# Expert 0 of a mixture-of-experts kernel: the half tile of rows turned with all 128 rows, and the turns between the second products of tiles 3 and 4 placed later

## The chip, the cores and the metric

The kernel runs on one core of one Trainium2 chip. The metric is the device time of one execution in microseconds (us). Three timed runs of the kernel before gave 525.79, 527.39 and 529.98 us, median 527.39 us; the profiled execution described below took 526.51 us.

## The reference

An attention layer with gates (8 heads of 40, 4 sequences of 768 steps) makes 3072 rows of 320 numbers. Those rows go through a mixture of 8 experts, two per row. All arithmetic is fp32.

```
logits = x @ w_gate
noisy_logits = logits + np.log1p(np.exp(x @ w_noise)) * noise
top2 = np.argpartition(-noisy_logits, 2, axis=1)[:, :2]
...
for e in range(E):
    for k in range(2):
        mask = top2[:, k] == e
        h = np.maximum(x[mask] @ w1[e], 0.0)          # 320 -> 1024
        out[mask] += top2_w[mask, k, None] * (h @ w2[e])   # 1024 -> 320
```

What the change touches lies in expert 0's part: picking its rows, turning them so that TensorE can contract over the 320 features, and the second product `h @ w2`.

## The kernel before

The first 130 us or so compute the attention in 24 units of 128 rows and write the rows to memory (`rows`). The routing of the last units runs on VectorE while expert 0 has already begun. After that, TensorE goes through experts 0 to 7 in program order.

Every fp32 product is made from parts: an operand is split into a high part and a low part (`xh` and `xl` for the rows, `w1h`/`w1l` and `w2h`/`w2l` for the weights, `hx` for both parts of the hidden values), and three products are summed in PSUM.

**Tiles.** An expert's rows lie in `XG`, tile t of 128 rows in `XG[:, t]`. Expert 0 and a few others have 832 rows: tiles 0 to 5 are full and tile 6 has 64 rows (`rows_of(6)` is 64). Expert 0 is worked in three pieces, as its rows become known: tiles 0 to 2, tiles 3 and 4, tiles 5 and 6. `XG` has no second copy: expert 1's tile t is gathered into the place of expert 0's. All of `XG` was set to zero early in the kernel (line 898).

**Gather (line 781).** GpSimd issues one indirect DMA per tile, which picks the tile's rows from memory by a list of row numbers (`tok`). In the stretch of the change seven are issued in a row: expert 0's tiles 5 and 6, then expert 1's tiles 0, 1, 2, 3 and 4. The same queue of GpSimd has carried expert 1's weights shortly before (lines 1135 and 1136).

**Turn (`transpose_x`, lines 807 to 816).** Three matmuls against the identity (`cs`) turn one tile's 3 x 128 feature columns into a PSUM bank (line 811). ScalarE copies the bank to `xh` (line 813), then VectorE subtracts for the low parts (lines 814 and 815), which frees the bank. The banks for turns come in the order `xt`, `s0`, `xt`, `s1` (function `bank`, line 738); there is one `xt` bank, and two buffers each of `s0` and `s1`. Tile 6 is turned with 64 rows and 64 columns.

**First product (`mm1`, line 1006).** For each of 8 blocks f of 128 hidden values, eight matmuls; ScalarE applies the relu and writes the high part (line 1017), VectorE the low part (line 1020).

**Second product (`mm2`, lines 1029 to 1050).** For one tile, 8 blocks j, each of three matmuls with 320 columns (lines 1036, 1037, 1038) into bank `o` or `st`. Block j needs the hidden values of f = j from ScalarE and VectorE. The argument `between` names a tile to turn behind block j. At the end VectorE scales the bank into `y` (line 1049), and `put` issues a scatter-add of `y` to the output from GpSimd (line 1059). A tile of 64 rows has 8 blocks of two matmuls (lines 1044 and 1045).

**Order.** Each engine works through its own instructions in the order written here. In the stretch of the change that order is, on TensorE: `mm1` of tiles 3 and 4, `mm2(0, 3)` into bank `o` with three turns between its blocks, `mm2(0, 4)` into bank `st` with two, `mm1` of tiles 5 and 6 with two turns, `mm2(0, 5)`, the turn of expert 1's tile 5, `mm2(0, 6)`, the turn of expert 1's tile 6, and then `mm1` of expert 1. In line 1149 the number before a colon is the block j behind which the turn stands, the number after it the tile: 5 and 6 are expert 0's tiles, 0, 1 and 2 are already expert 1's.

Of the kernel before, what the change touches and what calls it, by code (L numbers as in the profile page):

```python
# [64 lines left out]
def build(ctx, tc, qk, vk, og, fi, noise, wgn, w1, w2, cst, ce, out):  # L65
    nc = tc.nc
    V, A, P, T, SP = nc.vector, nc.scalar, nc.gpsimd, nc.tensor, nc.sync
# [11 lines left out]
    ident = cs[:, C_ID:C_ID + 128]  # L79
# [47 lines left out]
    XG = early.tile([128, 7, RW], F32, name="xg")  # L127
# [276 lines left out]
    CB3 = (0, 128, DM - 128)  # L404
# [17 lines left out]
    def l_part(i):  # L422

        t = XTB if i < NU else psum.tile([128, 512], F32, name="st")
        u = i - 2
        if 0 <= u < NU:
            for j in range(3):
                T.matmul(t[:, LGC:LGC + 16], XS[u][:, j, :], wgt[:, j, :], start=(j == 0), stop=(j == 2))
        return t
# [303 lines left out]
    def bank(use):  # L733

        n = dict(h=("s0", "s1", "e"), x=("xt", "s0", "xt", "s1"), y=("st", "o"))[use]
        turn[use] += 1
        name = n[turn[use] % len(n)]
        return psum.tile([128, 512], F32, name=name, bufs=2 if name in ("s0", "s1") else 1)
# [22 lines left out]
    def token(e, t):  # L761
        return TOK[0:rows_of(t), TC * e + t:TC * e + t + 1]
# [3 lines left out]
    def weigh(e, h=None):  # L766

        if not h:
            GW[e] = rt.tile([128, 7], F32, name="gw", bufs=2)
            GW[e, 2] = rt.tile([128, 7, 2], F32, name="gw2", bufs=2)  # L770
        t = tiles(e, h)
        n = slice(t[0], t[-1] + 1)
        V.tensor_mul(GW[e, 2][:, n], XG[:, n, DM:DM + 2], KM[:, TC * e + n.start:TC * e + n.stop])
        V.tensor_add(GW[e][:, n], GW[e, 2][:, n, 0], GW[e, 2][:, n, 1])
# [23 lines left out]
    def tiles(e, h=None):  # L798
        if h is None:
            return range(7 if is_long(e) else 6)  # L800
        c = parts(e)[h]
        return range(c.start // 128, -(-c.stop // 128))

    def rows_of(t):
        return 128 if t < 6 else 64

    def transpose_x(t, b=None):
        n = rows_of(t)
        ps = (bank("x") if b is None else b).rearrange("p (j t) -> p j t", j=4)[:, 0:3]
        for j in range(3):  # L810
            T.transpose(ps[:, j, 0:n], XG[0:n, t, CB3[j]:CB3[j] + 128], ident[0:n, 0:n])
        c = slice(128 * t, 128 * t + n)
        A.activation(XH[:, :, c], ps[:, :, 0:n], AF.Copy)  # L813
        V.tensor_sub(XL[:, :, c], ps[:, 0:2, 0:n], XH[:, 0:2, c].bitcast(F32))
        V.tensor_sub(XH[0:64, 2, c], ps[64:128, 2, 0:n], XH[64:128, 2, c].bitcast(F32))  # L815
# [7 lines left out]
    while i < NU - LEAD:  # L823
# [48 lines left out]
        t = l_part(i)  # L872
# [45 lines left out]
    for t, name in zip(tiles(0, 0), ("s", "e", "st")):  # L918
        shape = [128, 2, 512] if name == "s" else [128, 512]
        b = psum.tile(shape, F32, name=name, bufs=2 if name == "s" else 1)  # L920
        transpose_x(t, b[:, 0] if name == "s" else b)
    t = l_part(u)
# [9 lines left out]
    t = l_part(u)  # L932
# [96 lines left out]
    def mm2(e, t, b="y", between={}):  # L1029
        n = rows_of(t)  # L1030
        ps = bank(b)[:, 0:DM]
        y = m2.tile([128, DM], F32, name="y", bufs=TA + 1)
        if n == 128:
            c = slice(128 * t, 128 * t + 128)
            for j in range(8):
                T.matmul(ps, HH[:, j, c], W2H[:, j], start=j == 0, stop=False)  # L1036
                T.matmul(ps, HH[:, j, c], W2L[:, j], start=False, stop=False)  # L1037
                T.matmul(ps, HLO[:, j, c], W2H[:, j], start=False, stop=j == 7)  # L1038
                if j in between:
                    transpose_x(between[j])  # L1040
        else:

            for j in range(8):
                T.matmul(ps, HT[:, j], W2H[:, j], start=j == 0, stop=False)
                T.matmul(ps, HT[:, j], W2L[:, j], start=False, stop=j == 7)
            A.activation(y[0:n], ps[n:128], AF.Copy)
            V.tensor_add(y[0:n], y[0:n], ps[0:n])
            ps = y
        V.tensor_scalar(y[0:n], ps[0:n], GW[e][0:n, t:t + 1], None, op0=OP.mult)  # L1049
        return y  # L1050
# [4 lines left out]
    def put(e, t, y):  # L1055
        n = rows_of(t)

        P.memset(gap, 0.0)
        st = P.indirect_dma_start(out=out, out_offset=bass.IndirectOffsetOnAxis(ap=token(e, t), axis=0),  # L1059
                                  in_=y[0:n], in_offset=None, compute_op=OP.add)  # L1060
        for o in puts.setdefault(e, []):
            tc.declare_no_dep(st.ins, o.ins, reason="an expert has a token once")
        puts[e].append(st)
# [55 lines left out]
    for k, (l, r) in enumerate(((HH, W2H), (HLO, W2H), (HH, W2L))):  # L1119
        for n in range(24):  # L1120
            t, j = divmod(n, 8)
            T.matmul(sums[t], l[:, j, 128 * t:128 * t + 128], r[:, j], start=k == 0 and j == 0, stop=k == 2 and j == 7)
            if k == 1 and n % 4 == 0 and 4 <= n < 20:
                low_w2(n // 4 + 3)
            if n % 2:
                wipe()
                advance((0.27, 0.0, 0.27 if n < 14 else 0.0)[k])
            if k == 2 and j == 7:
                held[t] = m2.tile([128, DM], F32, name="y", bufs=TA + 1)
                A.activation(held[t], sums[t], AF.Copy, scale=GW[0][:, t:t + 1])  # L1130
            if k == 2 and n in (14, 19):
                transpose_x(tiles(0, 1)[n // 19])
# [13 lines left out]
    gather(1, ts=tiles(0, 1))  # L1146
    for t in tiles(0, 1):
        put(0, t - 3, held[t - 3])
        put(0, t, mm2(0, t, "y", {0: 5, 3: 6, 6: 0} if t == 3 else {2: 1, 5: 2}))
    weigh(0, 2)  # L1150
    gather(1, ts=tiles(0, 2))
    side = split_w1(V)
# [10 lines left out]
    for t in tiles(0, 2):  # L1163
        y = mm2(0, t)
# [84 lines left out]
    with tc.If(most > NT):  # L1249
# [23 lines left out]
        with tc.If(most > BLK):  # L1273
            V.memset(ec, 0.0)
            with tc.For_i(0, NE, 1) as e:
                weights(e)
                with tc.For_i(0, NCH, 1) as c:
# [8 lines left out]
                    for r in range(2):  # L1286
                        x = xf[:, DM * r:DM * r + DM]
                        t = XD.rearrange("(r c p) d -> r c p d", r=2, c=NCH)[r, bass.ds(c, 1)]
# [88 lines left out]
```

## Time and profile before

| | |
|---|---|
| median of three timed runs | 527.39 us (525.79 to 529.98) |
| the profiled execution, its own time | 526.51 us |
| its span, first to last instruction | 524.7 us (1.8 us lie around it) |
| TensorE busy | 504.5 us of the span |
| VectorE, ScalarE, GpSimd busy | 339.6, 247.8, 228.0 us |
| granted TensorE clock, mean | 0.983 |

PE is TensorE's matmul stream and PEld its weight loads, DVE is VectorE, ACT ScalarE, POOL GpSimd. In a timeline row stand the start in us from the beginning of the span, the length, the engine, the line, the operation with what it writes and reads, the shape, and how many were merged; a bracket gives the idle time of the engine just before and what ended it. The end of a matmul is modelled by the profiler, so the step between starts is the better measure of what one costs. Tile names lose their numbers in the profile, so `s` stands for both `s0` and `s1`.

### The profile page before, as it was taken

The numbers are of one execution on the slowest core, as the hardware profiler recorded it, in microseconds if no ns is written. First come the engines' busy times: TensorE is split into PE (matmuls) and PEld (weight loads), VectorE is DVE, ScalarE is ACT, GpSimd is POOL, SyncE is SP. The second block draws the span as 40 slices with busy tenths as digits, with TensorE's granted clock in tenths as the row PEclk, the third lists the DMA queues.
The fourth block names the chain that finished last, engine by engine and source line by source line (L and its number), as shares of the span: only waits on it lengthen the run. The fifth ranks groups of instructions, "written<-read, shape, count | busy, mean of one in ns | idle before, by whom it ended". The sixth has DMA issues, their size and how long they took to land.

```text
span 524.7 us, 13163 instructions
## 1 busy us (share of the span) xinstructions
PE 504.5 (96%) x5052; PEld 476.1 (91%) x5053; DVE 339.6 (65%) x963; ACT 247.8 (47%) x567; POOL 228.0 (43%) x298
## 2 busy tenths in 40 slices
PE   8899998999999899999999999999999999999993
PEld 4788887988988898999999999999999999999993
DVE  7787989999897476854764584376548347545310
ACT  8678877888623255432541454054325415515300
POOL 7356665365114657055315714550562254151042
PEclk9589999999999999999999999999999999999998
DMA  5788787777758446078239406831861593272033
GB/s 161 189 235 258 203 237 210 209 207 223 270 194 256 91 66 211 17 186 204 62 78 277 94 19 152 215 91 48 251 109 51 112 247 85 64 166 25 2 39 41
DMA packets 51669, 76.80 MB, mean 146 GB/s; under 512 B 10809, under 2 KB 42048, under 8 KB 51600
## 3 DMA queue, kind: packets, MB, share of 16 engines
q1 hardware_dynamic: 38816, 50.32, 32.3%
q0 software_dynamic: 12784, 25.57, 23.3%
q8 instruction: 42, 0.69, 0.5%
q14 instruction: 27, 0.22, 0.1%
HBM read 52.27 MB, written 17.48 MB: 133 GB/s over the span
## 4 chain that ended last, share of the span: by engine, by line
PE 78%; DVE 12%; ACT 5%; DMA 2%; issue 1%; POOL 0%; SPq 0%; POOLq 0%; DVEq 0%
PE s L1006 23%; PE e L1006 11%; PE o L1037 5%; PE o L1036 5%; PE o L1038 5%; PE st L1037 5%; PE st L1036 5%; PE st L1038 5%; PE o L385 3%; DVE p L362 2%; PE s L348 2%; PE e L325 2%; DVE ob L639 2%; PE st L376 1%; DVE kd L356 1%
## 5 line engine op out<-in xcount | busy, mean ns | idle before, releaser
L1059 POOL DMA_INDIRECT y_out<-y,tok x53 | 87.1, 1643 | 190.7 <-DVE y L1049 190.0
L1017 ACT ACTIVATE hx<-s 128x384 fp32r<-128x384 f32 (+5 forms) x91 | 44.4, 488 | 108.1 <-PE s L1006 67.1
L1006 PE MATMUL s<-xh,w1h 128*128 128x384 f32 (+5 forms) x273 | 76.7, 338 | 0.0
L1020 DVE SCALAR_TENSOR_TENSOR hx<-s,hx 128x384 fp32r<-128x384 f32 (+3 forms) x91 | 48.1, 529 | 37.5 <-ACT hx L1017 31.5
L781 POOL DMA_INDIRECT xg<-rows,tok x53 | 57.8, 1090 | 24.2 <-issue 14.3
L1006 PE MATMUL s<-xh,w1l 128*128 128x384 f32 (+5 forms) x273 | 62.5, 336 | 0.1
L1037 PE MATMUL o<-w2l,hx 128*128 128x320 f32 x184 | 57.3, 312 | 0.0
L1036 PE MATMUL o<-w2h,hx 128*128 128x320 f32 x184 | 57.1, 310 | 0.0
L1038 PE MATMUL o<-w2h,hx 128*128 128x320 f32 x184 | 56.6, 307 | 0.0
L1037 PE MATMUL st<-w2l,hx 128*128 128x320 f32 x176 | 54.9, 312 | 0.0
L1036 PE MATMUL st<-w2h,hx 128*128 128x320 f32 x176 | 54.5, 310 | 0.0
L1038 PE MATMUL st<-w2h,hx 128*128 128x320 f32 x176 | 54.1, 307 | 0.0
L1006 PEld LDWEIGHTS s<-xh,w1h 128*128 128x128 f32 x273 | 48.9, 188 | 1.7 <-ACT xh L813 0.3
L1006 PEld LDWEIGHTS s<-xh,w1l 128*128 128x128 f32 x273 | 47.9, 188 | 1.7 <-DVE xh L815 0.3
L1017 ACT ACTIVATE hx<-e 128x384 fp32r<-128x384 f32 (+5 forms) x45 | 22.1, 491 | 52.4 <-PE e L1006 34.1
L1006 PE MATMUL s<-xl,w1h 128*128 128x384 f32 (+5 forms) x182 | 46.4, 336 | 0.0
L1049 DVE TENSOR_SCALAR y<-o,gw 128x320 f32<-128x320 f32 x23 | 12.7, 550 | 46.5 <-PE o L1038 46.4
L1049 DVE TENSOR_SCALAR y<-st,gw 128x320 f32<-128x320 f32 x22 | 12.1, 550 | 43.8 <-PE st L1038 43.8
L397 POOL TENSOR_TENSOR xr<-tm,vk 128x320 f32<-128x320 f32 x24 | 20.9, 872 | 41.2 <-ACT w L328 14.3
L1006 PE MATMUL e<-xh,w1h 128*128 128x384 f32 (+5 forms) x135 | 38.6, 340 | 0.0
L1038 PEld LDWEIGHTS o<-w2h,hx 128*128 128x128 f32 x184 | 34.7, 188 | 0.0
L1036 PEld LDWEIGHTS o<-w2h,hx 128*128 128x128 f32 x184 | 34.6, 188 | 0.1
(237 smaller groups left out, 1255.2 us busy)
## 6 DMA issues: line engine op xcount, KB each, us to landing
raw<-w_in SPq DMA_DIRECT2D x6, 1280.0 KB
qk<-qk_in SPq DMA_DIRECT2D x24, 256.0 KB
raw<-w_in SPq DMA_DIRECT2D x6, 1024.0 KB
y_out<-zrow SPq DMA_DIRECT2D x15, 320.0 KB
raw<-w_in SPq DMA_DIRECT2D x17, 256.0 KB
vk<-vk_in POOLq DMA_DIRECT2D x24, 162.0 KB
vk<-vk_in SPq DMA_DIRECT2D x24, 162.0 KB
vk<-og_in SPq DMA_DIRECT2D x24, 160.0 KB
```

What stands on the lines that cost most here:

```text
L325: T.matmul(ps, LE[j][0:KE, c, 64 - 64 * p:192 - 64 * p], RE[j][0:KE, p, :, c * L:c * L + L], start=True, stop=True)
L385: T.matmul(OQ[u][half[p], h, :], PP[u][n, p, h, :], VK[u % 4][p][n, h * 41:h * 41 + 41], start=True, stop=True)
L397: P.tensor_mul(XR[u], tm.rearrange("p h d -> p (h d)"), SG[u % 4])
L781: P.indirect_dma_start(out=XG[0:rows_of(t), t], out_offset=None, in_=XD[0:n], in_offset=bass.IndirectOffsetOnAxis(ap=token(e, t), axis=0), ...
L1006: T.matmul(ps[:, 0:n], l, r, start=i == 0, stop=i == len(ops) - 1)
L1017: A.activation(hi, x, AF.Relu)
L1020: V.scalar_tensor_tensor(lo, top[0], 0.0, top[1].bitcast(F32), op0=OP.max, op1=OP.subtract)
L1036: T.matmul(ps, HH[:, j, c], W2H[:, j], start=j == 0, stop=False)
L1037: T.matmul(ps, HH[:, j, c], W2L[:, j], start=False, stop=False)
L1038: T.matmul(ps, HLO[:, j, c], W2H[:, j], start=False, stop=j == 7)
L1049: V.tensor_scalar(y[0:n], ps[0:n], GW[e][0:n, t:t + 1], None, op0=OP.mult)
L1059: st = P.indirect_dma_start(out=out, out_offset=bass.IndirectOffsetOnAxis(ap=token(e, t), axis=0), in_=y[0:n], in_offset=None, compute_op= ...
```

## The change

Two edits in expert 0's code, nothing else. The turn of any tile uses all 128 rows and 128 columns of `XG[:, t]`; only tile 6 had fewer before. ScalarE and VectorE still read just the 64 columns that hold rows. And the turns inside the second products of tiles 3 and 4 move: in tile 3 from behind blocks 0, 3 and 6 (tiles 5, 6 and expert 1's 0) to behind blocks 4 and 7 (tiles 5 and 6); in tile 4 from behind blocks 2 and 5 (expert 1's tiles 1 and 2) to behind blocks 1, 3 and 5 (expert 1's tiles 0, 1 and 2).

```
         for j in range(3):
-            T.transpose(ps[:, j, 0:n], XG[0:n, t, CB3[j]:CB3[j] + 128], ident[0:n, 0:n])
+            T.transpose(ps[:, j], XG[:, t, CB3[j]:CB3[j] + 128], ident)
...
     for t in tiles(0, 1):
         put(0, t - 3, held[t - 3])
-        put(0, t, mm2(0, t, "y", {0: 5, 3: 6, 6: 0} if t == 3 else {2: 1, 5: 2}))
+        put(0, t, mm2(0, t, "y", {4: 5, 7: 6} if t == 3 else {1: 0, 3: 1, 5: 2}))
```

No engine gets more or fewer instructions; GpSimd's and the DMA queues' order is the same. On TensorE, at the start of the second product of tile 3 before the change (`o` is its bank, `s1_3361` and `xt_3377` are the turned tiles 5 and 6; a bracket names the engines or DMA queues whose signals the instruction waits for):

```order
L1036 MATMUL o_3356<-w2h_121,hx_2802 128x320 [waits DVE_49,Activation_49]
L1037 MATMUL o_3356<-w2l_123,hx_2802 128x320
L1038 MATMUL o_3356<-w2h_121,hx_2802 128x320
L811 MATMUL s1_3361<-cs_66,xg_122 128x128 [waits DMASW7_49,DVE_49]
L811 MATMUL s1_3361<-cs_66,xg_122 128x128 x2
L1036 MATMUL o_3356<-w2h_121,hx_2802 128x320 [waits Activation_49]
```

The same turn in the changed kernel stands behind the fifth block, and that of tile 6 (`xt_3389`, now 128 columns) behind the last, right ahead of tile 4's product in bank `st`:

```order
L1036 MATMUL o_3356<-w2h_121,hx_2802 128x320 [waits Activation_49]
L1037 MATMUL o_3356<-w2l_123,hx_2802 128x320
L1038 MATMUL o_3356<-w2h_121,hx_2802 128x320 [waits DVE_49]
L811 MATMUL s1_3373<-cs_66,xg_122 128x128 [waits DMASW7_49]
L811 MATMUL s1_3373<-cs_66,xg_122 128x128 x2
...
L1038 MATMUL o_3356<-w2h_121,hx_2802 128x320 [waits DVE_49]
L811 MATMUL xt_3389<-cs_66,xg_122 128x128 [waits DMASW0_49,PE_49]
L811 MATMUL xt_3389<-cs_66,xg_122 128x128 x2
L1036 MATMUL st_3401<-w2h_121,hx_2802 128x320
```

The turn of tile 5 waits for the DMA queue that its gather uses; four more blocks now stand ahead of it. In tile 4's product after the change, `s0_3409` and `xt_3422` are expert 1's tiles 0 and 1:

```order
L1038 MATMUL st_3401<-w2h_121,hx_2802 128x320
L811 MATMUL s0_3409<-cs_66,xg_122 128x128 [waits DMASW1_49]
L811 MATMUL s0_3409<-cs_66,xg_122 128x128 x2
L1036 MATMUL st_3401<-w2h_121,hx_2802 128x320
L1037 MATMUL st_3401<-w2l_123,hx_2802 128x320
L1038 MATMUL st_3401<-w2h_121,hx_2802 128x320
L1036 MATMUL st_3401<-w2h_121,hx_2802 128x320
L1037 MATMUL st_3401<-w2l_123,hx_2802 128x320
L1038 MATMUL st_3401<-w2h_121,hx_2802 128x320
L811 MATMUL xt_3422<-cs_66,xg_122 128x128 [waits DMASW2_49,DVE_49,Activation_49]
L811 MATMUL xt_3422<-cs_66,xg_122 128x128 x2
```

Between the two turns that share bank `xt` (tile 6, then expert 1's tile 1) stand four blocks and one turn now; before the change it was seven blocks and one turn. On VectorE the scaling of tile 3's result (line 1049) came behind the low parts of tile 6 and of expert 1's tile 0 (`s0_3393`):

```order
L814 TENSOR_TENSOR xl_2668<-xt_3377,xh_2667 128x2x64 [waits Activation_49]
L815 TENSOR_TENSOR xh_2667<-xt_3377,xh_2667 64x64
L814 TENSOR_TENSOR xl_2668<-s0_3393,xh_2667 128x2x128 [waits Activation_49]
L815 TENSOR_TENSOR xh_2667<-s0_3393,xh_2667 64x128
L1049 TENSOR_SCALAR y_3357<-o_3356,gw_2806 128x320 [waits PE_49]
```

After the change it stands between them, so that it no longer waits for expert 1's tile 0:

```order
L814 TENSOR_TENSOR xl_2668<-xt_3389,xh_2667 128x2x64 [waits Activation_49]
L815 TENSOR_TENSOR xh_2667<-xt_3389,xh_2667 64x64
L1049 TENSOR_SCALAR y_3357<-o_3356,gw_2806 128x320
L814 TENSOR_TENSOR xl_2668<-s0_3409,xh_2667 128x2x128 [waits Activation_49]
L815 TENSOR_TENSOR xh_2667<-s0_3409,xh_2667 64x128
```

## Rows read from the trace of the kernel before

**Rows 1.** The page's head, its first part (busy time, share of the span, instructions) and the first line of its fourth (the chain of work that ended last, by engine).

```profile
span 524.7 us, 13163 instructions
PE 504.5 (96%) x5052; PEld 476.1 (91%) x5053; DVE 339.6 (65%) x963; ACT 247.8 (47%) x567; POOL 228.0 (43%) x298
PE 78%; DVE 12%; ACT 5%; DMA 2%; issue 1%; POOL 0%; SPq 0%; POOLq 0%; DVEq 0%
```

**Rows 2.** Busy time by stretch: the stretch and its length, then busy us and instructions of PE, PEld, DVE, ACT and POOL, the granted clock, the DMA engines' busy share, GB/s.

```profile
165.00:169.00 4.00, 4.00 (x37) 4.00 (x36) 3.07 (x18) 1.53 (x4) 2.07 (x2) 1.00 1.01 330
169.00:172.00 3.00, 1.52 (x13) 1.29 (x12) 0.85 (x2) 0.40 (x2) 2.19 (x3) 1.00 0.34 100
176.00:181.00 5.00, 4.39 (x33) 4.15 (x32) 2.67 (x8) 1.70 (x4) 2.18 (x3) 1.00 0.41 70
181.00:186.00 5.00, 5.00 (x48) 5.00 (x47) 4.60 (x20) 2.22 (x7) 4.31 (x6) 1.00 0.54 67
215.00:300.00 85.00, 85.00 (x527) 83.37 (x526) 47.76 (x120) 31.23 (x65) 37.78 (x39) 1.00 0.56 140
400.00:500.00 100.00, 100.00 (x626) 100.00 (x625) 53.80 (x116) 37.23 (x79) 28.10 (x31) 1.00 0.39 92
```

**Rows 3.** TensorE's timeline through the second products of tiles 3 and 4, from the last matmul of the first product to the next first product.

```profile
169.09 0.28 PE L1006 MATMUL s<-xh,w1h 128*128 128x256 f32 x1
169.21 0.31 PE L1036 MATMUL o<-w2h,hx 128*128 128x320 f32 x1
...
169.50 0.31 PE L1038 MATMUL o<-w2h,hx 128*128 128x320 f32 x1
171.29 0.52 PE L811 MATMUL s<-cs,xg 128*128 128x128 f32 x3 [1.48 <-DMA xg<-rows,tok]
171.56 0.39 PE L1036 MATMUL o<-w2h,hx 128*128 128x320 f32 x1
...
172.54 0.31 PE L1036 MATMUL o<-w2h,hx 128*128 128x320 f32 x1
...
173.07 0.40 PE L811 MATMUL xt<-cs,xg 64*128 64x64 f32 x3
173.40 0.41 PE L1036 MATMUL o<-w2h,hx 128*128 128x320 f32 x1
...
173.94 0.31 PE L1036 MATMUL o<-w2h,hx 128*128 128x320 f32 x1
...
174.38 0.31 PE L1036 MATMUL o<-w2h,hx 128*128 128x320 f32 x1
...
174.83 0.49 PE L811 MATMUL s<-cs,xg 128*128 128x128 f32 x3
175.08 0.39 PE L1036 MATMUL o<-w2h,hx 128*128 128x320 f32 x1
...
175.60 0.31 PE L1036 MATMUL st<-w2h,hx 128*128 128x320 f32 x1
...
176.78 0.31 PE L1038 MATMUL st<-w2h,hx 128*128 128x320 f32 x1
177.70 0.52 PE L811 MATMUL xt<-cs,xg 128*128 128x128 f32 x3 [0.61 <-ACT xh L813]
177.97 0.39 PE L1036 MATMUL st<-w2h,hx 128*128 128x320 f32 x1
...
180.60 0.36 PE L1006 MATMUL e<-xh,w1h 128*128 128x192 f32 x2
```

**Rows 4.** The gather of tile 5 in the chain of work that ended last: start, us, what (for a DMA from its issue to its landing).

```profile
166.53 4.63 DMA xg<-rows,tok
```

**Rows 5.** GpSimd's timeline: the first and the last of the seven gathers issued in a row, of tile 5 and of expert 1's tile 4 (the third to the fifth of them are expert 1's tiles 0 to 2).

```profile
166.53 1.06 POOL L781 DMA_INDIRECT xg<-rows,tok  x1 [5.86 <-DVE over L662]
...
174.46 1.01 POOL L781 DMA_INDIRECT xg<-rows,tok  x1 [0.30 <-issue]
```

**Rows 6.** ScalarE's timeline: the relu of the last block ahead of tile 3's second product, the copies of the turned tiles 5 and 6, and the copy of expert 1's tile 2.

```profile
170.88 0.38 ACT L1017 ACTIVATE hx<-s 128x256 fp32r<-128x256 f32 x1 [1.86 <-PE s L1006]
172.39 0.49 ACT L813 ACTIVATE xh<-s 128x384 fp32r<-128x384 f32 x1 [1.12 <-PE s L811]
176.70 0.33 ACT L813 ACTIVATE xh<-xt 128x192 fp32r<-128x192 f32 x1 [3.82 <-PE o L1038]
...
179.91 0.49 ACT L813 ACTIVATE xh<-s 128x384 fp32r<-128x384 f32 x1 [0.81 <-PE s L811]
```

**Rows 7.** VectorE's timeline: the two instructions for the low parts of tile 6, the second of which frees bank `xt`.

```profile
177.06 0.29 DVE L814 TENSOR_TENSOR xl<-xt,xh 128x128 fp32r<-128x128 f32 x1 [3.42 <-ACT xh L813]
177.37 0.23 DVE L815 TENSOR_TENSOR xh<-xt,xh 64x64 fp32r<-64x64 f32 x1
```

**Rows 8.** TensorE's timeline: the turn of expert 1's tile 2 (128 rows), and the turn of expert 1's tile 6 (64 rows) with its neighbours.

```profile
179.39 0.49 PE L811 MATMUL s<-cs,xg 128*128 128x128 f32 x3
...
194.29 0.31 PE L1044 MATMUL st<-w2h,hx 128*128 128x320 f32 x1
194.44 0.31 PE L1045 MATMUL st<-w2l,hx 128*128 128x320 f32 x1
194.68 0.40 PE L811 MATMUL s<-cs,xg 64*128 64x64 f32 x3
195.00 0.73 PE L1006 MATMUL s<-xh,w1h 128*128 128x512 f32 x2
```

## The prediction

> **What bounds the kernel now.** I read the page's head and chain first: TensorE is busy for 504.5 of 524.7 us and holds 78% of the chain that ended last [rows 1]. So a change counts here by what it does to TensorE's stream. The busy time by stretch then shows where that stream has holes. From 181 us on there are none that the stretches shown would reveal (5.00 of 5.00, 85.00 of 85.00, 100.00 of 100.00); the stretch 169 to 172 has 1.52 us busy out of 3, and 176 to 181 has 4.39 out of 5 [rows 2]. Both lie in the second products of tiles 3 and 4, which the change rearranges. The timeline names them: ahead of the turn of tile 5 the engine sat idle until a gather landed, and ahead of the turn of expert 1's tile 1 until ScalarE's copy of line 813, because both that turn and tile 6's use the one bank `xt` [rows 3].
>
> The steps between starts give the prices. A block of three matmuls takes 174.38 - 173.94 = 0.44 us. Without a wait the turn of tile 5 would have started one third of a block after 169.50, at 169.65; it started at 171.29, so the first wait costs 1.64 us. In the same way the second costs 177.70 - 176.93 = 0.77 us [rows 3]. The reader should see that the idle times in brackets (1.48 and 0.61) are smaller, since the modelled end of a matmul lies about 0.16 us behind the next possible start.
>
> **Edit 1, 128 rows for tile 6.** A turn of 128 rows put between blocks stretches the step around it from 0.44 to 0.70 us (174.38 to 175.08) and the next from 0.44 to 0.52 (175.08 to 175.60), so it costs 0.34. The 64-row turn stretches them to 0.86 (172.54 to 173.40) and 0.54 (173.40 to 173.94) and costs 0.52 [rows 3]. Its own three matmuls take less (0.40 against 0.49); it loses more at its edges. Turned with 128 rows it gives 0.18 us. The same holds for expert 1's tile 6: from the end of the step after 194.44, at 194.59, to 195.00 it takes 0.41, against 0.26 for the full turn up to the next block [rows 3, 8], so 0.15 more. Nothing is added elsewhere: ScalarE and VectorE read the same 64 columns, and the other 64 rows were zeroed long before, so there is no new wait.
>
> The Trainium skill speaks against this edit: TensorE: Matmul & The Clock Gate, section Back-to-back issue gap, has the step of a matmul grow with its columns (columns / 2.4 ns plus 2.5 at the full clock). As an estimate from that page, 64 more columns would cost 3 x 27 ns = 0.08 us per turn and the edit would lose 0.16 us in all. The trace bears the page out for the three matmuls alone, and not for the stream around them.
>
> **Edit 2, the turn of tile 5 four blocks later.** TensorE now issues five blocks from 169.21 before it: 169.21 + 5 x 0.443 = 171.42 (0.443 is the mean step of 0.44 before rounding). The gather landed at 166.53 + 4.63 = 171.16 [rows 4], so the 1.64 us are covered by work that had to be done anyway, with 0.26 us to spare. If the gather landed later by more than that, the rest would be a wait again. The blocks that move ahead need the hidden values of f up to 4 first, and f = 7 last; the last relu was done at 171.26 [rows 6], and block 7 comes at about 172.6. No hole there.
>
> **Edit 2, the other turns.** The schedule without waits: tile 6 at 171.42 + 0.34 + 3 x 0.443 = 173.09, expert 1's tile 0 at 174.32, tile 1 at 175.54, tile 2 at 176.77, the next first product at 178.0, against 180.60 before. Are the rows there? Tile 6 was turned at 173.07 without a DMA wait, so it is. The seven gathers were issued (174.46 - 166.53) / 6 = 1.32 us apart [rows 5]. With tile 5's 4.63 us as an estimate for each, expert 1's tiles 0, 1 and 2 land at 173.8, 175.1 and 176.4: ahead of their turns by 0.5, 0.4 and 0.3. I take this as an upper bound of the landing, since tile 5 was issued while the DMA engines were full (share 1.01 up to 169) and the later ones when they were not (0.34) [rows 2]. Bounds: no wait, or some tenths.
>
> Is bank `xt` free at 175.54? It was freed 177.60 - 176.70 = 0.90 us after ScalarE's copy began [rows 6, 7], and the next turn came 0.10 later. An undisturbed copy begins 0.52 us after its turn (179.39, 179.91) [rows 6, 8], so the bank needs 1.52 us; the two turns stand 2.45 us apart. Then the 0.77 us go too, with 0.9 to spare. The catch is that tile 6's copy did not begin 0.52 us after its turn, but 3.63 us (173.07, 176.70), though ScalarE was idle for 3.82 us [rows 3, 6]. TensorE's signal came late. That is the open price, and it decides between the first case and the first rival.
>
> **Sum.** 1.64 + 0.77 + 0.18 + 0.15 = 2.74 us less. All of it passes to the end, since TensorE has no later hole to swallow it. The granted clock is 1.00 (2.4 GHz) in the stretch with the wait as in its neighbours [rows 2], so the clock neither gives nor takes. GpSimd's scatter of tile 3 waits for line 1049, which moves forward; expert 1's later gathers stand behind that scatter and can only come earlier. The profiled execution took 526.51 us; 526.51 - 2.74 = 523.8. The median of the three runs lies 0.88 above it, and I forecast against the median: 527.39 - 2.74 = **524.7 us**.
>
> **Rivals.** *The late signal comes again.* Three signals in a row were late here: the relu at 170.88 (1.79 us after 169.09), tile 5's copy (1.10), tile 6's (3.63). The first was late ahead of any 64-row turn, which speaks for something in this stretch of time that the change leaves alone. Against it: the third and longest follows the 64-row turn, which goes. If tile 6's copy begins at 176.70 again, bank `xt` is free at 177.60, the turn of tile 1 starts at 177.70 as before, but with four blocks behind it in place of five: 0.44 is gained there (tile 6's 0.18 is lost in the wait), 0.15 at expert 1's tile 6, 0.6 in all: 526.8. From a copy that begins 1.45 us after its turn on (2.45 - 1.00), each us is one us of wait.
>
> *A gather lands later.* The slack is 0.26 us for tile 5 and 0.3 to 0.5 by estimate for three others. A landing 1 us later gives 0.74 back: 525.4. For it: the queue was full of weights just before. Against it: nothing ahead of the gather changes.
>
> *The wider turns lose.* If the edges that I charged to 64 rows belong to their neighbours, edit 1 gives nothing or costs 0.09 each: 525.0 to 525.2. The page of the Trainium skill named above would have it so.
>
> *Slower.* Bank `xt` is asked for 2.45 us after tile 6's turn, where it was 4.63 (173.07 to 177.70). If tile 6's signal comes later still, the wait outgrows what is gained: the break-even is a turn of tile 1 at 178.29, a copy that begins at 177.29, 4.2 us after the turn. At 5.5 us it is 1.3 us slower: 528.7. For it speaks the 3.63 seen; against it that every other signal in the rows came faster.
>
> **How the numbers follow.** 0.50 for the forecast, 0.30 for the late signal (wholly or in part), 0.11 for a gather, 0.06 for the wider turns, 0.03 for slower. The cases lie between 524.7 and 528.7, and the three runs of the kernel before spread from 1.6 under to 2.6 over their median, more than the whole effect. I take 1.9 below the forecast and 1.0 above the late-signal case: 522.8 to 527.8. A measurement of this kernel can tell about 1% (5.3 us) from no change, and no case reaches that; what is left for either side is the spread of the runs: faster 0.04, same 0.94, slower 0.02.
>
> **What would show it.** Right: no idle before the turn of tile 5, which starts at about 171.4; the first product of tiles 5 and 6 starts at about 178.0; steps around tile 6's turns of 0.70 and 0.52. The late signal: ScalarE's copy from `xt` at about 176.7 and TensorE idle before the turn of expert 1's tile 1, with the first product at about 180.2. Wrong altogether: a new hole in TensorE's stream after 181, or a first product at 180.6 or later.

## The result, and the profile after

The changed kernel took 531.33 us (median of 14 runs, 526.35 to 533.62), the kernel before 528.01 us in the same session (14 runs, 525.79 to 531.15). The ratio is 1.0064, 95% interval 1.0042 to 1.0086: 2.2 to 4.5 us slower, where 2.74 us less had been forecast. The profiled execution took 533.29 us. Ratios here and below leave out single executions that took over 1.5% more than the kernel's fastest, and the profile of `e7_tile5_early` (535.12 us) is of such an execution, so less rests on it.

The page's span, its first row of busy time and the first line of its chain answer to [rows 1], and a row of TensorE's waits names what is new:

```profile
span 531.5 us, 13162 instructions
PE 505.6 (95%) x5052; PEld 478.0 (90%) x5053; DVE 339.4 (64%) x963; ACT 247.6 (47%) x567; POOL 227.9 (43%) x298
PE 79%; DVE 10%; DMA 3%; issue 2%; ACT 2%; POOL 2%; another core or an unknown queue 1%; SPq 1%; POOLq 0%; DVEq 0%
```

```profile
PE xt L811 <- ACT xh L813: 3.4, 1, 3.4
```

The span is 6.8 us longer than in [rows 1], but not all of that is the change: `mm2(0, 3)` starts at 173.67 instead of 169.21, 4.46 us later, for reasons that lie ahead of every edited line. So I measure the stage, from the start of `mm2(0, 3)` to the next first product: 180.60 - 169.21 = 11.39 us before [rows 3], 187.56 - 173.67 = 13.89 after, 8.79 forecast. TensorE's timeline of the stage after, against [rows 3] (only the turns, what stands behind them, and the ends):

```profile
173.67 0.31 PE L1036 MATMUL o<-w2h,hx 128*128 128x320 f32 x1
...
175.87 0.49 PE L811 MATMUL s<-cs,xg 128*128 128x128 f32 x3
...
177.53 0.49 PE L811 MATMUL xt<-cs,xg 128*128 128x128 f32 x3
177.78 0.39 PE L1036 MATMUL st<-w2h,hx 128*128 128x320 f32 x1
...
178.76 0.49 PE L811 MATMUL s<-cs,xg 128*128 128x128 f32 x3
...
183.56 0.87 PE L811 MATMUL xt<-cs,xg 128*128 128x128 f32 x3 [3.43 <-ACT xh L813]
...
184.77 0.47 PE L1038 MATMUL st<-w2h,hx 128*128 128x320 f32 x1
185.04 0.47 PE L1036 MATMUL st<-w2h,hx 128*128 128x320 f32 x1
...
185.84 0.84 PE L811 MATMUL s<-cs,xg 128*128 128x128 f32 x3
...
187.56 0.36 PE L1006 MATMUL e<-xh,w1h 128*128 128x192 f32 x2
```

Up to 178.76 everything runs as forecast: tile 5 is turned 2.20 us into the stage without a wait, tile 6 at 3.86, expert 1's tile 0 at 5.09 (forecast: 2.21, 3.88, 5.11). Then TensorE stands idle for 3.43 us in front of the turn of expert 1's tile 1, and when it goes on a matmul steps by 0.27 us (184.77 to 185.04) instead of 0.15. The windows show the same as granted clock (columns as in [rows 2]):

```profile
173.00:176.00 3.00, 3.00 (x25) 3.00 (x24) 0.74 (x2) 0.77 (x2) 2.39 (x3) 1.00 0.43 130
176.00:181.00 5.00, 4.13 (x31) 3.85 (x29) 0.11 (x1) 0.00 (x0) 3.90 (x6) 1.00 0.47 130
181.00:186.00 5.00, 2.44 (x10) 2.42 (x11) 3.13 (x9) 1.69 (x4) 2.68 (x4) 0.75 0.29 44
186.00:189.00 3.00, 3.00 (x24) 3.00 (x22) 1.50 (x6) 0.82 (x2) 1.86 (x4) 0.85 0.71 85
```

ScalarE did nothing at all from 176 to 181 (0.00 us busy), while three turns lay ready for its copy. Its timeline, against [rows 6] (`remote` in a bracket: the profile could put the releaser to no engine of this core):

```profile
175.27 0.39 ACT L1017 ACTIVATE hx<-s 128x256 fp32r<-128x256 f32 x1 [1.79 <-PE s L1006]
181.05 0.49 ACT L813 ACTIVATE xh<-s 128x384 fp32r<-128x384 f32 x1 [5.40 <-remote]
182.57 0.33 ACT L813 ACTIVATE xh<-xt 128x192 fp32r<-128x192 f32 x1 [1.02 <-remote]
182.80 0.48 ACT L813 ACTIVATE xh<-s 128x384 fp32r<-128x384 f32 x1
```

Tile 5's copy begins 5.18 us after its turn (175.87), tile 6's 5.04 us after (177.53). VectorE follows at once, and its second subtraction is what frees bank `xt`, 0.09 us before the turn at 183.56 (compare [rows 7]):

```profile
183.24 0.23 DVE L815 TENSOR_TENSOR xh<-xt,xh 64x64 fp32r<-64x64 f32 x1
```

GpSimd, as in [rows 5], issues its seven gathers in a row over the same time. Here the first and the last of the seven:

```profile
171.00 1.06 POOL L781 DMA_INDIRECT xg<-rows,tok  x1 [5.88 <-DVE over L662]
...
178.94 1.01 POOL L781 DMA_INDIRECT xg<-rows,tok  x1 [0.30 <-issue]
```

The sum of the stage. Tile 6's copy begins 182.57 - 173.67 = 8.90 us into it, before 176.70 - 169.21 = 7.49 [rows 3, 6]: 1.41 later, and the turn of tile 1 with it (9.89 against 8.49). Four blocks stand behind that turn in place of five, -0.44. The lower clock: from tile 1's turn to tile 2's 2.28 us and on to the first product 1.72, where the forecast's schedule has 1.22 and 1.23, so +1.55. In all 1.40 - 0.44 + 1.55 = 2.51, as measured (13.89 - 11.39 = 2.50). The second wide turn gives 0.15 back, so 2.35 us net, inside the 2.2 to 4.5 of the timed runs.

### The profile page after: what moved, and what is told of

It is laid out like the page before. It is cut to its first block, busy times and chain, and to the rows that moved or that the text cites. A ratio compares the mean times of both kernels' runs of the same rounds, so it can differ in the third digit from the quotient of the medians.

```text
span 531.5 us, 13162 instructions
## 1 busy us (share of the span) xinstructions
PE 505.6 (95%) x5052; PEld 478.0 (90%) x5053; DVE 339.4 (64%) x963; ACT 247.6 (47%) x567; POOL 227.9 (43%) x298
## 4 chain that ended last, share of the span: by engine, by line
PE 79%; DVE 10%; DMA 3%; issue 2%; ACT 2%; POOL 2%; another core or an unknown queue 1%; SPq 1%; POOLq 0%; DVEq 0%
PE s L1006 24%; PE e L1006 12%; PE o L1037 5%; PE o L1036 5%; PE st L1037 5%; PE o L1038 5%; PE st L1036 5%; PE st L1038 5%; PE o L385 3%; PE s L348 2%; DVE p L362 2%; PE st L376 2%; PE e L325 2%; PE xt L428 1%
## 5 line engine op out<-in xcount | busy, mean ns | idle before, releaser
L1036 PE MATMUL st<-w2h,hx 128*128 128x320 f32 x176 | 55.3, 314 | 0.0
L1038 PE MATMUL st<-w2h,hx 128*128 128x320 f32 x176 | 54.4, 309 | 0.0
L385 PE MATMUL o<-vk,p 128*64 128x41 f32 (+2 forms) x768 | 29.8, 233 | 5.6 <-issue 3.2
L1038 PEld LDWEIGHTS o<-w2h,hx 128*128 128x128 f32 x184 | 34.7, 188 | 0.0
```

The source lines that it names most:

```text
L385: T.matmul(OQ[u][half[p], h, :], PP[u][n, p, h, :], VK[u % 4][p][n, h * 41:h * 41 + 41], start=True, stop=True)
```

## The experiments

**One edit alone.** The first two kernels each undo one of the edits. Kernel `e1_rows_only` keeps the old places:

```
-        put(0, t, mm2(0, t, "y", {4: 5, 7: 6} if t == 3 else {1: 0, 3: 1, 5: 2}))
+        put(0, t, mm2(0, t, "y", {0: 5, 3: 6, 6: 0} if t == 3 else {2: 1, 5: 2}))
```

> Only the first edit: tile 6 is turned with 128 rows, all turns stay where they were. Theory A (TensorE's signals to ScalarE come late in this stretch, and the change hurts by asking for bank xt sooner): about 0.3 us less than the kernel before, ratio 0.999 to 1.000, ScalarE's copy of tile 6 still about 3.4 us behind its turn. Theory B (turning 128 rows is what costs): the loss of the whole change, ratio 1.005 or more.

528.72 us (12 runs) against 528.52 before; ratio 1.0009, interval 0.9979 to 1.0038: no change that can be seen, as theory A has it for the time. Kernel `e2_places_only` keeps the 64-row turn:

```
-            T.transpose(ps[:, j], XG[:, t, CB3[j]:CB3[j] + 128], ident)
+            T.transpose(ps[:, j, 0:n], XG[0:n, t, CB3[j]:CB3[j] + 128], ident[0:n, 0:n])
```

> Only the second edit: the turns move, tile 6 keeps 64 rows. Theory A: the whole loss, ratio 1.005 to 1.008, a wait of some 3 us before the turn of expert 1's tile 1 and a granted clock under 1 behind it. Theory B: no loss, ratio 1.000 or less.

530.68 us; ratio 1.0038, interval 1.0008 to 1.0069, and 1.96 us above `e1_rows_only` by the medians. So a loss comes with edit 2 also where tile 6 keeps its 64-row turn; whether it is the whole loss (1.0064) the intervals don't tell. The wait before expert 1's tile 1 is 1.77 us where theory A expected some 3 and the granted clock stays at 1.00 where it expected less; the turns ahead came later here. TensorE and ScalarE of `e2_places_only`:

```profile
175.67 0.55 PE L811 MATMUL s<-cs,xg 128*128 128x128 f32 x3 [1.29 <-DMA xg<-rows,tok]
...
181.95 0.52 PE L811 MATMUL xt<-cs,xg 128*128 128x128 f32 x3 [1.77 <-ACT xh L813]
```

```profile
179.43 0.49 ACT L813 ACTIVATE xh<-s 128x384 fp32r<-128x384 f32 x1 [5.38 <-PE s L811]
180.95 0.33 ACT L813 ACTIVATE xh<-xt 128x192 fp32r<-128x192 f32 x1 [1.03 <-remote]
```

Two things are to be seen. A gather that landed later than the forecast's 4.63 us made the turn of tile 5 wait in spite of the four blocks. And the copies are late again, though tile 5's turn came late too: they begin at a moment, not at a distance from their turns. In `e1_rows_only` they were on time (0.80 and 0.88 us behind the turns of tiles 5 and 6, where theory A expected 3.4 for tile 6), but there TensorE had waited 3.05 us for tile 5's gather and ran at the lower clock:

```profile
172.14 0.77 PE L811 MATMUL s<-cs,xg 128*128 128x128 f32 x3 [3.05 <-DMA xg<-rows,tok]
```

```profile
172.00:176.00 4.00, 3.86 (x17) 3.85 (x18) 0.72 (x2) 0.50 (x2) 3.20 (x5) 0.57 0.48 136
```

**Is bank `xt` what turns lateness into loss?** Kernel `e3_own_bank` is the changed kernel with expert 1's tile 1 turned into a buffer of `s0`:

```
-                    transpose_x(between[j])
+                    transpose_x(between[j], psum.tile([128, 512], F32, name="s0", bufs=2)
+                                if between[j] == 1 and not turn.update(x=turn["x"] + 1) else None)
```

> The changed kernel, but expert 1's tile 1 is turned into the second buffer of bank s0 in place of xt. Theory A: the wait of 3.4 us before that turn is gone, the clock stays at 1.00, the first product of tiles 5 and 6 starts up to 1 us late for tile 6's copy, and the time falls to 1.0 to 2.5 us under the kernel before (ratio 0.995 to 0.998). If what costs is the place of the turns and not the bank, the ratio stays at 1.004 to 1.007.

527.41 us; ratio 0.9984, interval 0.9953 to 1.0015. That excludes the 1.004 to 1.007 expected if the places were what costs; the gain that theory A expected isn't clear of noise. The stage takes 182.18 - 171.68 = 10.50 us. The copies are as late as ever (179.14, 5.20 us after the turn at 173.94), but no turn waits for a bank, and the granted clock stays at 1.00. What is left are two idle times of TensorE at the very moments at which the copies come out (179.14, 180.65), with no releaser that the profile can name (the copy of tile 5, then TensorE):

```profile
179.14 0.49 ACT L813 ACTIVATE xh<-s 128x384 fp32r<-128x384 f32 x1 [5.41 <-remote]
```

```profile
179.10 0.27 PE L811 MATMUL s<-cs,xg 128*128 128x128 f32 x1 [0.62 <-issue]
...
180.53 0.31 PE L1036 MATMUL st<-w2h,hx 128*128 128x320 f32 x1 [0.71 <-issue]
```

**Who holds the signals?** Kernel `e4_gathers_later` issues all of expert 1's gathers behind tile 4's scatter, and turns its tiles 0 to 2 in `mm2(0, 5)`, tiles 3 and 4 behind that:

```
-                    gather(1, ts=tiles(0, 0))
...
-    gather(1, ts=tiles(0, 1))
-        put(0, t, mm2(0, t, "y", {4: 5, 7: 6} if t == 3 else {1: 0, 3: 1, 5: 2}))
+        put(0, t, mm2(0, t, "y", {4: 5, 7: 6} if t == 3 else {}))
-    gather(1, ts=tiles(0, 2))
+    gather(1)
...
+        y = mm2(0, t, between={1: 0, 3: 1, 5: 2} if t == 5 else {})
```

> The changed kernel, but expert 1's gathers are issued, and its rows turned, only behind the second product of tile 4, so that GpSimd issues two gathers in place of seven in the stretch. Theory A1 (the run of gathers holds back TensorE's signals): ScalarE's copies of tiles 5 and 6 begin 0.3 to 0.6 us behind their turns in place of 4.8. Theory A2 (the signals are late for a reason of TensorE's own or of this place in the program): still 3 us or more. The time itself tells nothing, since expert 1 waits for its gathers.

533.78 us in a single run. The copies of tiles 5 and 6 are on time now (0.52 us behind the turn at 175.99), and the late ones stand where the gathers went (issued from 185.65 to 193.71): the turn of tile 1 at 190.75 is copied 5.02 us later. Counted from the start of the first gather there (185.65), the copies of expert 1's tiles 0, 1 and 2 begin at 7.24, 10.12 and 11.61 us. Two rows of ScalarE:

```profile
176.51 0.49 ACT L813 ACTIVATE xh<-s 128x384 fp32r<-128x384 f32 x1 [1.44 <-PE s L811]
...
195.77 0.49 ACT L813 ACTIVATE xh<-xt 128x384 fp32r<-128x384 f32 x1 [2.39 <-remote]
```

Is it the rows that arrive in `XG`, or GpSimd's issuing? Two kernels fetch expert 1's tiles 0 to 4 by plain DMAs in plain order, so that expert 1 works on other rows; SyncE issues them in `e5_rows_by_sync`, GpSimd in `e6_rows_by_pool` (`P` in place of `SP`):

```
-                    gather(1, ts=tiles(0, 0))
+                    [SP.dma_start(XG[:, x], XD[128 * x:128 * x + 128]) for x in (0, 1, 2)]
...
-    gather(1, ts=tiles(0, 1))
+    [SP.dma_start(XG[:, x], XD[128 * x:128 * x + 128]) for x in (3, 4)]
```

> The changed kernel, but expert 1's tiles 0 to 4 are fetched by plain DMAs that SyncE issues (the same bytes into the same places, the rows in plain order, so expert 1 works on other rows than the reference). Theory A1a (it is GpSimd's issuing of indirect DMAs that holds back TensorE's signals): ScalarE's copy of tile 5 begins 0.3 to 0.6 us behind its turn, and there is no wait of over 1 us before the turn of expert 1's tile 1. Theory A1b (it is the rows landing in xg): the copies stay 3 us or more late.

531.44 us in a single run. Tile 5's gather landed very late here, so the stage has a hole of another kind, but all five copies are on time (0.52 to 0.58 us behind their turns):

```profile
179.54 0.55 PE L811 MATMUL s<-cs,xg 128*128 128x128 f32 x3 [3.20 <-DMA xg<-rows,tok]
```

> As the run before, but GpSimd issues the plain DMAs. A1a in its narrow form (only the indirect form of issue): copies 0.3 to 0.6 us behind their turns. A1a in its wide form (any issue on GpSimd's queue) and A1b: 3 us or more late.

523.96 us in a single run. TensorE has no hole in the stage, which takes 178.33 - 169.54 = 8.79 us, the forecast's own figure. The copies of tiles 5 and 6 begin 0.58 and 0.53 us behind turns at 171.76 and 173.48:

```profile
172.34 0.49 ACT L813 ACTIVATE xh<-s 128x384 fp32r<-128x384 f32 x1 [2.21 <-PE s L811]
174.01 0.33 ACT L813 ACTIVATE xh<-xt 128x192 fp32r<-128x192 f32 x1 [1.17 <-PE xt L811]
```

So rows that arrive are not enough: in `e6_rows_by_pool` the DMA engines were busier (share 0.68 from 172 to 176) than in the changed kernel (0.47 from 176 to 181), and the copies were on time. `e5_rows_by_sync` doesn't test that, since SyncE issued at 159.75 and 166.80 and the DMA share was 0.00 from 180 to 183. Nor do the two tell whether it takes the indirect form: GpSimd was done with its plain DMAs at 172.00, before the first copy, and its whole run of issues (5.1 us from 166.86) was shorter than that of seven gathers (9.0 us):

```profile
170.90 1.10 POOL L1146 DMA_DIRECT2D xg<-rows  x2
```

**Is it a matter of time since the first gather?** Kernel `e7_tile5_early` takes the new places with tile 5 back behind block 0 (`{0: 5, 7: 6}` for tile 3), and `e8_before_again` is one more profiled run of the kernel before.

> The changed kernel with one number put back: tile 5 is turned behind block 0, as before. Theory A (signals are let out at a few moments of this stretch, one turn at each, so that tile 5's turn coming late pushes tile 6's copy to the next): tile 6's copy begins about 1.5 us earlier than in the changed kernel, counted from the first gather (10.2 us after it in place of 11.6), the wait before expert 1's tile 1 shrinks below 2 us, and the ratio is 0.997 to 1.002. If only the shorter distance between the two turns in bank xt counts: the copy is as late as in the changed kernel and the ratio stays at 1.004 to 1.007.

529.43 us; ratio 1.0023, interval 0.9998 to 1.0048, between the two ranges that were expected. Tile 6's copy came 11.57 us after the first gather, where theory A expected 10.2, but the profile can't decide for the rival: tile 5's gather was late and the granted clock 0.68 from 181 to 186, so tile 6's turn itself came only 10.35 us after the first gather, and its copy 1.22 us behind it:

```profile
184.53 0.49 PE L811 MATMUL xt<-cs,xg 128*128 128x128 f32 x3
```

```profile
185.75 0.33 ACT L813 ACTIVATE xh<-xt 128x192 fp32r<-128x192 f32 x1 [5.17 <-PE xt L811]
```

> The kernel before, once more, for a second profile of it. Every theory: a wait of 1 to 3 us before the turn of tile 5. Theory A: tile 6's copy again 2 us or more behind its turn, if TensorE runs at the full clock there; a copy that is on time would make the late signal of the first profile a chance event.

528.93 us in a single run. Tile 6's copy is late again (3.48 us behind its turn), so the first profile was no chance event. All times in us since the start of the first of the seven gathers:

| kernel | first gather starts at | relu f = 7 | tile 5's turn | tile 5's copy | tile 6's turn | tile 6's copy |
|---|---|---|---|---|---|---|
| before | 166.53 | 4.35 | 4.76 | 5.86 | 6.54 | 10.17 |
| `e8_before_again` | 168.90 | 3.63 | 4.87 | 5.81 | 6.65 | 10.13 |
| `e7_tile5_early` | 174.18 | 4.32 | 5.35 | 5.91 | 10.35 | 11.57 |
| after | 171.00 | 4.27 | 4.87 | 10.05 | 6.53 | 11.57 |
| `e2_places_only` | 169.33 | 4.33 | 6.34 | 10.10 | 8.15 | 11.62 |
| `e3_own_bank` | 169.00 | 4.35 | 4.94 | 10.14 | 6.66 | 11.65 |

What waits for TensorE starts at about 4.3 (3.63 in `e8_before_again`), 5.8, 10.1 and 11.6 us after the first gather, wherever the turns stand. The late copies of `e4_gathers_later` and, below, of `e9_two_gathers_after_put` and `e10_tiny_fill_between` add about 7.2 and 8.7, so the moments lie some 1.45 us apart; why they do is open. That places the loss: before, tile 5's copy gets the moment at 5.8 and tile 6's the one at 10.1; after, tile 5's takes 10.1 and tile 6's 11.6, and bank `xt` is freed 1.4 us later. That the one is left with 11.6 because the other took 10.1 is a reading of the table; `e7_tile5_early` was to test it and didn't. Why tile 5 misses 5.8 the turn's time alone doesn't tell: `e7_tile5_early` turned it at 5.35 and was copied on time, the changed kernel at 4.87 was not. What differs is what TensorE ran since its last first product: three matmuls and an idle time (before, e7 and e8) against fifteen matmuls without a hole (after and e3). No run tests that difference by itself.

**Room between the gathers.** If the run is the cause, breaking it up must free the signals. `e10_tiny_fill_between` puts a fill of 32 numbers on GpSimd ahead of each of the seven gathers, `e12_gathers_spaced` two fills of 128x512 ahead of those of expert 1's tiles 0, 1 and 2 (the buffer is made larger for it), both in the changed kernel:

```
+            if e == 1 and t < 3:
+                P.memset(gap[0:128], 0.0)
+                P.memset(gap[0:128], 0.0)
             P.indirect_dma_start(out=XG[0:rows_of(t), t], out_offset=None, in_=XD[0:n],
```

> The changed kernel with a fill of 32 numbers on GpSimd ahead of each of the seven gathers (0.1 us each), as stands ahead of each scatter. Theory that it is gathers directly behind one another that hold the signals: the copy of tile 5 begins 0.5 us after its turn, no wait for bank xt, 525 to 528. Rival, each gather holds whatever stands between: the copies come as in the changed kernel (5.2 us after tile 5's turn), wait for xt of about 3.4 us, 530 to 533.

535.6 us in a single run: tile 5's copy at 181.97, 3.76 us behind its turn, tile 6's 5.01 us behind, a wait of 3.4 us for bank `xt` again, a stage of 13.80 us. The gathers still start 1.32 us apart, so the fill only took the place of an idle time, though tile 5's copy came sooner (8.64 us after the first gather, tile 6's 11.55).

> The changed kernel with about 1.1 us of fills on GpSimd ahead of each of the gathers of expert 1's tiles 0, 1 and 2, so that these come some 2.4 us apart in place of 1.32. They land later: the turn of expert 1's tile 0 waits for its gather, by an estimate 1 to 3 us, which is not what this run is for. Theory that a run without room between gathers holds the signals: the copies of tiles 5 and 6 begin within 1 us of their turns. Rival, any gather under way holds them: tile 5's copy begins 2 to 5 us after its turn again.

526.37 us in a single run: gathers 2.43 us apart, the first four copies 0.53 to 0.56 us behind their turns, and waits for two gathers that now come late. The stage takes 10.21 us.

Kernel `e9_two_gathers_after_put` tries the other way, on top of `e3_own_bank`: five gathers in the run, those of tiles 3 and 4 behind tile 3's scatter.

```
-    gather(1, ts=tiles(0, 1))
...
+        if t == 3:
+            gather(1, ts=tiles(0, 1))
...
-        if f in (2, 4):
-            transpose_x(tiles(0, 1)[f // 4])
+        if f in (4, 6):
+            transpose_x(tiles(0, 1)[f // 6])
```

> The kernel of e3 (expert 1's tile 1 turned into a bank of its own), and in it the gathers of expert 1's tiles 3 and 4 are issued behind tile 3's scatter instead of in the run of seven, with their two turns two blocks f later in the next first product. Theory: the run of indirect gathers holds TensorE's signals back until it ends. With five gathers in the run (some 6.6 us in place of 9.2) the copy of tile 5 comes no later than in e3 and the copies behind it come together some 2 us sooner after their turns; TensorE has fewer holes, second product of tile 3 to the next first product 8.9 to 9.8 us (e3: 10.50, e6: 8.79), ratio to before 0.994 to 0.998. Rival: the hold starts again with the two gathers that come after the scatter, so that the hole only moves; then 526.5 to 528, ratio 0.997 to 1.001.

526.32 us; ratio 0.9962, interval 0.9931 to 0.9992: faster than the kernel before, and not to be told from `e3_own_bank`. The copies of tiles 5 and 6 still come 2.31 and 2.15 us behind their turns, but 7.19 and 8.69 us after the first gather (171.52), 2.95 sooner than in `e3_own_bank` for a run that is 2 x 1.32 = 2.6 us shorter. Nothing waits for them, and the stage takes 182.94 - 174.20 = 8.74 us. The two copies:

```profile
178.71 0.49 ACT L813 ACTIVATE xh<-s 128x384 fp32r<-128x384 f32 x1 [3.25 <-PE xt L811]
180.21 0.33 ACT L813 ACTIVATE xh<-xt 128x192 fp32r<-128x192 f32 x1 [1.01 <-PE s L811]
```

The last three set the room between gathers and the places against each other: `e13_one_fill` and `e14_after_two_fills` are the changed kernel with one fill or two (the latter is the kernel of `e12_gathers_spaced`), `e15_before_two_fills` is the kernel before with two.

> The changed kernel with one fill of about 0.55 us on GpSimd ahead of the gathers of expert 1's tiles 0, 1 and 2 (gathers some 1.9 us apart). If that is room enough: copies 0.5 us after their turns, no wait for bank xt, less waiting for gathers than with two fills; second product of tile 3 to the next first product 8.8 to 9.4 us, 524 to 526, ratio to before 0.992 to 0.997. If it is not: tile 5's copy comes 2 us or more after its turn and TensorE waits for xt again, 527 to 531.

524.70 us against 528.13; ratio 0.9922, interval 0.9895 to 0.9949, the fastest of the kernels timed 12 times. GpSimd, ScalarE's first two copies and TensorE's turns of the same two tiles in `e13_one_fill`:

```profile
172.00 0.54 POOL L782 MEMSET gap<- 128x512 f32 x1
172.70 1.03 POOL L783 DMA_INDIRECT xg<-rows,tok  x1 [0.16 <-issue]
173.73 0.54 POOL L782 MEMSET gap<- 128x512 f32 x1
174.43 1.01 POOL L783 DMA_INDIRECT xg<-rows,tok  x1 [0.17 <-issue]
```

```profile
175.03 0.49 ACT L815 ACTIVATE xh<-s 128x384 fp32r<-128x384 f32 x1 [2.15 <-PE s L813]
176.69 0.33 ACT L815 ACTIVATE xh<-xt 128x192 fp32r<-128x192 f32 x1 [1.17 <-PE xt L813]
```

```profile
174.50 0.49 PE L813 MATMUL s<-cs,xg 128*128 128x128 f32 x3
176.16 0.49 PE L813 MATMUL xt<-cs,xg 128*128 128x128 f32 x3
```

Gathers that start 1.73 us apart instead of 1.32 are enough: every copy begins 0.53 us behind its turn, TensorE waits ahead of no turn, and the stage takes 181.02 - 172.30 = 8.72 us.

> The kernel of e12 timed (the changed kernel, gathers of expert 1's tiles 0 to 2 some 2.4 us apart). Theory, the held signals were the whole loss: second product of tile 3 to the next first product 10.2 us as in the one look, against 11.39 before, ratio to before 0.996 to 0.999. Rival, part of the loss lies elsewhere: ratio above 1.001.

526.17 us; ratio 0.9960, interval 0.9932 to 0.9988; stage 10.21 us, with 0.92 us of waiting for expert 1's tile 2.

> The kernel before with the same two fills ahead of the same three gathers: old places, 64-row turn. Theory that the gathers hold the signals in the kernel before as well: the copies of tiles 5 and 6 begin 0.5 us after their turns, no wait for bank xt, the wait for tile 5's gather stays (some 1.6 us); second product of tile 3 to the next first product 10.6 to 11.0 us, and the time 0.3 to 0.8 us under that of the kernel before, above the changed kernel with the same fills by 0.4 to 1.2 us. Rival, the held signals have another cause: tile 6's copy begins about 10.1 us after the first gather again.

527.41 us; ratio 1.0004, interval 0.9975 to 1.0032. The copies are on time here too (0.55 and 0.62 us behind their turns) and bank `xt` costs nothing, but the gain of 0.3 to 0.8 us that I expected can't be seen. In its profile tile 5's gather landed 5.4 us after its issue, TensorE waited 2.10 us for it, the granted clock was 0.76 from 172 to 176, and the stage took 12.67 us. In `e1_rows_only` the copies were on time at the lower clock without any fill, so this run doesn't show that the gathers hold the signals in the kernel before as well; `e12_gathers_spaced` and `e13_one_fill` had the clock at 1.00.

The last two are the fair pair for the change: with the same two fills on both sides the changed kernel is 527.41 - 526.17 = 1.24 us faster by the medians, and the ratios to the kernel before (0.9960 and 1.0004) have intervals that overlap a little. The fills without the new places gain nothing that can be seen. The kernel before with one fill was not run.

## Why the prediction was wrong

- **The wait for tile 5's gather, 1.64 us.** Right in the profiled execution after: no wait, turn at 2.20 us of the stage. The "0.26 us to spare" came from one landing. In the profiles the turns that did wait for this gather began 4.8 to 8.2 us after its issue, and with tile 5 behind block 4 two kernels still waited (1.29 and 3.20). The rival "a gather lands later" is a matter of the execution.
- **The wait for bank `xt`, 0.77 us.** This is the step that failed: "Is bank `xt` free at 175.54?", answered with a copy 0.52 us behind its turn. The prediction named the catch and priced it under "Slower" (break-even at a copy 4.2 us behind the turn, 528.7 at 5.5), then gave it 0.03 because "every other signal in the rows came faster". The copy came 5.04 us behind, which by that price is 5.04 - 4.2 = 0.8 us slower; the rest of the 2.35 is the clock, below, which the price left out. The range also ended at 527.8, under the 528.7 of that case. What was missed is that the release is a moment that goes with the gathers, and the change leaves those where they are: a relu, a copy and another copy were late one behind the other [rows 6] over GpSimd's run of gathers [rows 5]. The rival "comes again" kept the moment 176.70 for tile 6, but not for what now stands ahead of it on ScalarE: with twelve more matmuls ahead of its turn, tile 5's copy came at that moment, and tile 6's at the next. The times are measured; that the one pushed the other is argued.
- **"The clock neither gives nor takes."** Wrong through the step above. After an idle time of 1.48 us [rows 3] the granted clock stayed at 1.00 [rows 2]; with 3.43 us it was 0.75 in the window that holds the idle time and 0.85 in the next, and TensorE's steps were 0.27 us, the 1.2 GHz level. That took 1.55 us.
- **Edit 1, 0.18 + 0.15.** The sizes held. Around tile 6's turn the steps are 177.78 - 177.09 = 0.69 and 178.31 - 177.78 = 0.53 (forecast 0.70 and 0.52), and the second wide turn takes 201.80 - 201.55 = 0.25 from its start to the next product, against 0.41 in [rows 8]:

```profile
201.55 0.49 PE L811 MATMUL s<-cs,xg 128*128 128x128 f32 x3
201.80 0.71 PE L1006 MATMUL s<-xh,w1h 128*128 128x512 f32 x2
```

  The whole-kernel time of `e1_rows_only` (0.9979 to 1.0038) is too wide to tell 0.33 us. The estimate from the Trainium skill (TensorE: Matmul & The Clock Gate, section Back-to-back issue gap) had the wider turns lose 0.16 us by their columns; the rows between blocks show the gain. The section gives that formula for a single matmul by itself and says that in a stream the weight loads set the spacing too, so the prediction stretched it.
- **The sum, 2.74 us.** The schedule without waits was right: `e6_rows_by_pool` took exactly 8.79 us for the stage and `e13_one_fill` 8.72. With one fill the changed kernel is 1 - 0.9922 = 0.8%, 4.1 us (2.7 to 5.5), under the kernel before, and that counts the fill with the change; with two fills on both sides it was 1.24 us, waits for late gathers included. So the 2.74 lies between two measurements and is confirmed by neither. That 4.1 is more I put down to the profile of before being a lucky one: the four profiled executions with the old places or nearly so (before, `e8_before_again`, `e1_rows_only`, `e15_before_two_fills`) have stages of 11.39, 11.36, 13.55 and 12.67 us, the longer ones by the late gather and the lower clock. That is argued from single profiles, not shown.

Shown is that the run of gathers back to back decides: spaced or replaced by a shorter run of plain DMAs, the copies come on time; moved, the lateness moves along. Not shown is whether plain DMAs for as long would do the same, nor by what way GpSimd's issuing keeps back a signal that TensorE sends to ScalarE. Only the fill was tried as a spacer, so whether a mere pause would do is open. About 1 us of the timed loss (3.4 against 2.35 from one profile) isn't assigned either.

## What to carry to other kernels

Where an engine idles with its input ready, look for what else runs at that moment, and ask whether the lateness belongs to the instruction or to the time; a lateness that belongs to the time does not move when the instruction moves, and what is placed closer behind it runs into it. Two uses of one bank need the distance of the latest copy that the trace shows, not of the undisturbed one. Here neither the change alone (1.0064) nor spaced gathers alone (1.0004, two fills) gained; the two together did (0.9922 with one fill, 0.9960 with two).

## What the runs showed of the hardware

- While GpSimd issued seven indirect gathers 1.32 us apart and TensorE streamed 320-column matmuls at the upper clock, what waits for TensorE was started up to 5.2 us behind its matmuls, at about 4.3, 5.8, 10.1 and 11.6 us after the first gather. With a fill of 0.54 us ahead of three of them (1.73 us apart) it was 0.53 us, and the last three gathers, 1.32 us apart again (176.16, 177.48, 178.79), held back none of `e13_one_fill`'s copies.
- Short runs hold a little: in `e4_gathers_later` and `e5_rows_by_sync`, with two gathers and a scatter in a row, the relu of f = 7 began 0.91 and 0.94 us after `mm2(0, 3)` had started, against 0.20 in `e13_one_fill`.
- It seems to need more than the run; one profile each speaks for that. In `e1_rows_only`, with the same seven gathers and TensorE at the lower clock, the copies were on time. And in the kernel before, seven gathers from 199.31 to 207.53 lie over the first product of expert 1, whose matmuls have 512 columns: its relus come every 1.87 us, and only one is late, by 0.43 us (208.80 - 206.50 = 2.30):

```profile
204.63 0.60 ACT L1017 ACTIVATE hx<-e 128x512 fp32r<-128x512 f32 x1 [0.91 <-issue]
...
206.50 0.60 ACT L1017 ACTIVATE hx<-s 128x512 fp32r<-128x512 f32 x1 [0.91 <-issue]
...
208.80 0.60 ACT L1017 ACTIVATE hx<-s 128x512 fp32r<-128x512 f32 x1 [1.34 <-PE s L1006]
```

- TensorE itself can stand still with them: in `e3_own_bank` it was idle for 0.62 and 0.71 us right up to the two moments at which the copies came out, the first time between two matmuls of one turn.
